# Four of sixteen x chunks transposed by TensorE instead of by the load, in a two-branch state-space kernel with a written-out order

## The chip, the cores and the metric

The kernel runs on one core of one Trainium2 chip. The metric is the time of one execution on the device in microseconds (us); of several executions the median is given. A difference of about 0.5% is what a measurement of this kernel can tell from no change.

## The reference

Two state-space layers over the same length S = 2048 and width D = 1024 are computed from separate inputs and set side by side in one output of 2048 x 2048.

```python
# branch A: short convolution of k, gate by v, long convolution, gate by q
kv = k_shift * v                      # k_shift: 4 shifted copies of k, weighted and summed
y  = irfft(rfft(kv, 2*S) * rfft(ssm_k, 2*S))[:S] + kv * ssm_D
a  = q * y
# branch B: diagonal complex recurrence
Bu = einsum("bld,pd->blp", x, B_bar)  # B_bar from Lambda, log_dt, B_re, B_im
for t in range(L): h = Lam_bar * h + Bu[:, t]; hs.append(h)
b  = 2 * einsum("blp,dp->bld", hs, Cmat).real + x * Dskip
out = concatenate([a, b], axis=-1)
```

## The kernel before

**One order for everything.** The kernel's work is cut into about 1,500 small tasks. A string, `ORDER`, names them one after the other, and the program walks through it (the loop over `ORDER.split()` at the end of `full_kernel`): each word calls the function of that task, which issues its instructions. Each engine takes its own instructions in this order, so the string sets five queues at once: TensorE, VectorE, ScalarE, GpSimd (half of the stores and swaps) and SyncE (all loads, some stores). A word such as `x.12:a52` is task x for chunk 12, into the working memory from unit 52 on; p is a PSUM bank, h one of three slots of the state, w one of three slots of weights. A task waits for its data and for what lay in its place before.

**Branch B** goes in 16 chunks of 128 time steps. Task x loads a chunk of x with a transposing DMA on SyncE (line 447), so that the width lies on the partitions. U (line 464) multiplies it with the tables BT, made at the start from B by transposes on TensorE (bT, line 415, 128 x 128 each, eight to a tile, against an identity) and a copy out of PSUM. ue copies U out of PSUM. VectorE then rotates (r1, line 487; r2, 498), scans twice (sc, 504), rotates back (r3, 487; r4, 510). cy carries the last column to the next chunk. y (line 520) or its form in four quarters yq (538) multiplies with CT and adds x * Dskip with one small matmul from the same transposed chunk; ye (556) copies out, and a store follows. Eight pieces of CT come by transposing loads (line 437), eight by TensorE and a copy on ScalarE (439).

**Branch A** does the long convolution as a Fourier transform in stages. am and hm are the first stages for kv and the filter; their results go to memory and come back re-sorted (lh, lk, line 676) as 16 units. For each unit stage 2 needs a table of weights, loaded by lw (line 671) into one of three slots `wslot`: sh and sk (line 687) read it first, and sa (line 725) last, after the product pr on VectorE (713) and the swap of rows sw or swp (707). Results are stored, come back (vl, 741), go through a3 (753), are copied out (a3e, 760), multiplied by q (qm, 762) and stored (763 on GpSimd, 764 on SyncE).

Most copies out of PSUM can stand on ScalarE or, with a v at the end of the task's name, on VectorE.

Of the kernel before, what the change touches and what calls it, by code (L numbers as in the profile page):

```python
# [16 lines left out]
BF16 = mybir.dt.bfloat16  # L17
# [55 lines left out]
ue.1.0:a34 bl.3.1:a19 bc.4.0 U.0.0.0:p5 U.0.0.1 bl.7.0:a41 bT.2.1:p4 bl.6.1:a12 U.0.2.0:p0 bT.3.1:p7 bc.5.0 U.0.2.1
bT.7.0:p6 stt ue.0.0:a24 bl.7.1:a20 bc.2.0 bc.2.1 x.2:a52 bT.6.1:p2 bT.7.1:p3 cl.1.0:a15 kp.-2 bT.3.0:p4 bc.7.0 kring
bc.3.1 x.3:a21 bc.3.0 U.1.2.1:p5 bc.7.1 U.1.2.0 cl.1.1:a37 U.1.1.1:p1 bc.6.1 U.1.1.0 cl.3.1:a14 U.0.3.1:p4 ue.0.2 ue.1.2
kvm.1:a16 z2 kvm.2:a42 U.0.3.0 rta kva.1 kva.2 z1 U.0.1.0:p7 kvb.1:a39 cT.1.0:p6 U.3.0.1:p3 ue.0.3 kvb.2:a12 U.0.1.1
ue.0.1 cc.1.0 cT.3.1:p0 vp.1:a27 kvm.0:a16 cl.0.1:a48 kvb.3:a26 kva.0 kvc.3 cc.3.1 ld_Q ue.1.1 vp.0:a40 kvb.0:a36
U.3.0.0 cx.5.1 cl.2.0:a13 U.3.2.0:p5 am.3.1:p7p2 ae.3.1.1:a19 r1.0:a29 kvc.2 U.3.2.1 ae.3.0.1 cl.0.0:a47 am.3.0:p6p4
cx.7.0 kvc.1 ae.3.1.0 ae.3.0.0 cT.1.1:p1 cl.2.1:a44 cT.0.1:p0 cT.0.0:p7 U.3.1.1:p2 cc.1.1 cx.6.0 U.3.3.1:p4 cl.3.0:a42
ue.3.2:a46 kp.2 cT.2.1:p5 U.3.1.0 gz r2.0:h1 kvc.0 ue.3.0 sc.0.0 sc.0.1 am.2.1:p1p3 cc.0.0 U.1.3.0:p7 cc.0.1 hl.0.1:a23  # L80
cT.3.0:p6 r3.0:a27 ue.3.1 U.3.3.0 ae.2.0.1:a40 U.1.3.1 cc.2.1 cc.3.0 U.2.0.1:p2 hl.1.0:a48 ae.2.1.1 am.0.0:p0p3 ue.3.3
ue.1.3 ae.0.0.0:a43 ae.0.1.0 am.0.1:p4p5 ae.0.1.1 r1.3:a15 U.2.0.0 ue.2.0:a36 am.1.1:p0p6 hl.0.0 r4.0 U.2.2.0:p1 hl.1.1
ae.0.0.1 ast.0 am.1.0:p2p7 ae.1.0.1:a45 U.2.2.1 cx.6.1 r2.3:h2 ast.3 hT.0.1:p4 r1.1:a27 hT.0.6:p3 ae.1.1.0 U.2.3.1:p7
kvm.4:a14 ae.1.1.1 ue.2.2 cx.4.1 ae.1.0.0 r2.1:h0 hd.0 am.2.0:p6p5 hc.0.1:a22 U.2.3.0 ae.2.1.0 ast.1 cx.7.1 hd.1 ue.2.3
cT.2.0:p1 ae.2.0.0 hT.0.3:p2 cc.2.0 hc.0.6:a32 U.2.1.0:p7 U.2.1.1 hc.0.3:a13 hT.0.7:p0 hm.0.6.1:p4p1 hT.0.4:p6 cx.4.0
cy.1 kva.4 y.0.0.0:p3 ue.2.1 ast.2 sc.1.1 hc.0.4:a28 sc.1.0 hc.0.7:a12 y.0.0.1 hm.0.4.0:p2p6 kvb.4:a31 he.0.6.1.0:a43
he.0.4.0.1:a29 he.0.4.0.0 he.0.6.1.1 hT.0.0:p5 cx.5.0 hT.0.5:p0 vp.2:a34 y.0.0.2 hT.0.2:p1 r3.1:a45 hc.0.0:a19
hm.0.6.0:p6p2 he.0.6.0.0 hm.0.4.1:p5p4 he.0.4.1.1 he.0.4.1.0 y.0.0.3 hst.0.6.1 y.0.1.0:p6 kp.3 ye.0.0:a25 hc.0.5:a14
kvc.4 hst.0.4.1 y.0.1.1 he.0.6.0.1 r4.1 y.0.1.2 hm.0.0.1:p0p5 hc.0.2:a20 hm.0.7.0:p4p7 he.0.7.0.1:a50 y.0.1.3 r1.2:a15
hst.0.4.0 he.0.0.1.1:a48 hm.0.0.0:p2p3 hm.0.5.1:p7p5 y.1.1.0:p1 hst.0.6.0 he.0.7.0.0 kvm.6:a38 he.0.0.1.0 he.0.0.0.1  # L90
y.1.1.1 he.0.5.1.0:a23 he.0.0.0.0 hm.0.5.0:p4p2 he.0.5.1.1 he.0.5.0.1 vp.3:a26 am.4.0:p0p7 ye.0.1 he.0.5.0.0
ae.4.1.0:a29 x.4:a32 kp.4 y.1.1.2 y.1.1.3 y.1.0.0:p6 r2.2:h1 ae.4.0.0 kva.6 hm.0.7.1:p0p3 ye.1.1:a28 hst.0.7.0
hm.0.3.0:p2p5 hm.0.3.1:p7p4 y.1.0.1 kvm.5:a14 he.0.7.1.0 ysp.0 he.0.7.1.1 am.4.1:p1p0 cy.2 kvb.6:a19 kva.5 kvc.6
he.0.3.1.1:a36 y.1.0.2 he.0.3.1.0 kvb.5:a25 hst.0.0.1 he.0.3.0.0 hm.0.1.0:p3p2 hl.2.0:a44 sc.2.1 hst.0.5.1 hl.2.1
# [24 lines left out]
ye.4.1:a11 kva.14 U.6.2.1:p1 kvc.13 am.13.1:p6p0 cy.5:h1 kva.12 ye.4.0 kvb.14:a3 lw.0:w0 ae.11.1.0 am.13.0:p5p3
ae.13.1.1:a9 kvc.15 U.8.3.0:p2 ae.13.0.0 ast.10 lh.3:a5 kvc.14 ae.11.0.0 ae.13.1.0 kvb.12:a20 ae.13.0.1 U.6.2.0  # L120
am.15.0:p3p0 am.14.1:p7p5 ae.14.0.1:a21 ae.15.0.0:a34 ae.15.1.0 U.8.3.1 ast.11 U.7.2.1:p4 r1.5:a45 ue.6.2 ae.14.1.1
am.15.1:p3p0 ae.15.1.1 kvc.12 am.14.0:p1p7 ast.13 ae.15.0.1 ae.14.1.0 x.10:a26 U.7.2.0 ae.14.0.0 r2.5 am.12.1:p5p0
lh.1:a32 ae.12.1.1:a45 U.9.0.1:p7 ae.12.0.1 am.12.0:p6p3 ae.12.1.0 ae.12.0.0 r1.6:a41 ue.7.2 ue.8.3:a38 U.9.0.0
ue.9.0:a30 U.8.1.1:p3 sc.5.0 sh.2:p5p4 sh.3:p0p1 she.3.0:a47 sc.5.1 she.2.1 ast.14 sh.7:p2p6 she.3.1 lh.0:a0 U.8.1.0
she.2.0 r2.6:h2 U.9.1.0:p0 U.8.2.0:p4 ysp.4 she.7.0:a11 she.7.1 ue.8.1 U.9.1.1 sh.1:p6p1 ast.12 sh.6:p7p5 sh.0:p2p3
# [63 lines left out]
def full_kernel(ctx, tc, A_q, A_k, A_v, A_shift_k, A_ssm_k, A_ssm_D, B_x, B_Lre, B_Lim, B_Bre, B_Bim,  # L189
                B_Cre, B_Cim, B_log_dt, B_Dskip, out):  # L190
    nc = tc.nc
# [252 lines left out]
    def x_(i):  # L444
        nm = "xm" if i in bounced else "xT"
        st[nm, i] = sb(1).rearrange("p (d t) -> p d t", d=ND)
        nc.sync.dma_start_transpose(st[nm, i], x[i * T:(i + 1) * T, :])
# [394 lines left out]
```

## Time and profile before

| what | us |
|---|---|
| three timed runs | 351.01, 348.97, 350.45; median 350.45 |
| profiled execution, whole | 352.94 |
| its span, first to last instruction | 351.0 |
| TensorE busy in the span | 332.9 |
| VectorE busy | 326.1 |
| ScalarE busy | 273.4 |
| mean granted clock of TensorE | 0.989 |

The profile is one execution. PE is TensorE, PEld its weight load, DVE VectorE, ACT ScalarE, POOL GpSimd, and SP (or SPq, its queue) SyncE. An x with a number counts instructions. A window's row gives its length, the busy time and count of each engine, the granted clock of TensorE, the mean busy share of the 16 DMA engines (packets that overlap can bring it over 1) and what they moved in GB/s. A row of the timeline gives start and length of a group of like instructions, and in brackets the idle time ahead of it and what ended that. A row of the waits gives us in all, times, and the longest.

### The profile page before, as it was taken

How to read it: one execution, taken by the hardware profiler on the slowest of the kernel's cores; microseconds unless marked ns; L12 is line 12 of the kernel's file. 1: busy time of each engine (PE TensorE's matmuls, PEld its weight loads, DVE VectorE, ACT ScalarE, POOL GpSimd, SP SyncE). 2: the span in 40 equal slices, each digit the busy share in tenths (PEclk: the TensorE clock that was granted, in tenths of full speed). 3: DMA queues.
4: the chain of work that ended last, by engine and by line, in shares of the span. 5: the costliest groups of instructions: out<-in, count | busy, mean ns of one | idle time of the engine just before them, and what ended most of it. 6: DMA issues, size and time to landing. Idle time of an engine off the chain costs nothing. (4 is left out here: it accounts for less than half of the span.)

```text
span 351.0 us, 11815 instructions
## 1 busy us (share of the span) xinstructions
PE 332.9 (95%) x5105; PEld 233.2 (66%) x5105; DVE 326.1 (93%) x261; ACT 273.4 (78%) x524; POOL 68.0 (19%) x110
## 2 busy tenths in 40 slices
PE   5989999999999999999999989999699999999991
PEld 2789888547856886689665565765575887754440
DVE  4999999999999999999999989999779999999961
ACT  6999999999999973798889769999378974235640
POOL 6000011343422552120111210031021122000020
PEclk9999999999999999999999999999899999999997
DMA  5999999898996888968998999898978898798996
GB/s 193 357 286 293 278 264 324 271 288 329 279 327 211 319 283 234 324 233 307 308 244 293 194 357 357 309 236 250 292 264 301 288 314 310 229 381 273 366 326 226
DMA packets 62880, 101.09 MB, mean 288 GB/s; under 512 B 29422, under 2 KB 31742, under 8 KB 62828
## 3 DMA queue, kind: packets, MB, share of 16 engines
q1 hardware_dynamic: 53228, 67.39, 66.1%
q0 software_dynamic: 9600, 32.95, 25.9%
q8 instruction: 40, 0.66, 0.8%
q14 instruction: 12, 0.10, 0.1%
HBM read 52.08 MB, written 33.55 MB: 244 GB/s over the span
## 5 line engine op out<-in xcount | busy, mean ns | idle before, releaser
L464 PEld LDWEIGHTS <-BT 128*128 128x128 bf16 x2048 | 118.4, 99 | 13.7 <-issue 9.2
L464 PE MATMUL bank<-arena,BT 128*128 128x128 bf16 x2048 | 126.0, 221 | 0.3 <-ACT BT L431 0.3
L538 PE MATMUL bank<-CT,gslot 64*64 64x512 bf16 x1408 | 88.2, 378 | 0.1
L504 DVE TENSOR_TENSOR_SCAN gslot<-rtab,gslot 128x1040 bf16<-128x1040 f32 x32 | 72.9, 2310 | 0.7
L538 PEld LDWEIGHTS <-gslot 64*64 64x64 bf16 x1408 | 38.8, 107 | 29.4 <-issue 1.4
L473 ACT CAST arena<-bank 128x512 bf16<-128x512 f32 x61 | 37.2, 642 | 14.0 <-PE bank L464 13.0
L613 ACT CAST arena<-bank 128x512 bf16<-128x512 f32 x64 | 36.6, 658 | 8.0 <-PE bank L607 5.3
L520 PE MATMUL bank<-CT,gslot 128*128 128x512 bf16 x160 | 39.4, 379 | 0.0
L696 ACT CAST arena<-bank 128x512 bf16<-128x512 f32 x62 | 33.4, 615 | 7.3 <-PE bank L687 5.7
L713 DVE TENSOR_TENSOR arena<-arena 128x4096 bf16<-128x4096 bf16 x16 | 36.5, 2285 | 2.3 <-ACT arena L473 1.6
L487 DVE TENSOR_TENSOR arena<-gslot,Z 128x4096 bf16<-128x4096 bf16 x16 | 36.6, 2288 | 0.9 <-PE bank L687 0.4
L703 ACT CAST arena<-bank 128x512 bf16<-128x512 f32 x60 | 33.7, 609 | 4.0 <-PE bank L687 2.6
L487 DVE TENSOR_TENSOR arena<-arena,Z 128x4096 bf16<-128x4096 bf16 x16 | 36.5, 2283 | 0.0
L733 ACT CAST arena<-bank 128x512 bf16<-128x512 f32 x60 | 32.7, 615 | 4.4 <-PE bank L725 4.4
L664 ACT CAST arena<-bank 128x512 bf16<-128x512 f32 x64 | 34.6, 635 | 1.7 <-PE bank L656 1.6
L587 DVE TENSOR_TENSOR arena<-arena 128x4096 bf16<-128x4096 bf16 (+3 forms) x16 | 29.9, 1880 | 0.0
L667 POOL DMA_DIRECT2D Ys_h<-arena x32 | 23.5, 737 | 28.6 <-ACT arena L664 26.1
L616 POOL DMA_DIRECT2D Ys_kv<-arena x16 | 11.1, 711 | 87.2 <-ACT arena L613 86.1
L687 PE MATMUL bank<-arena,wslot 64*64 64x512 bf16 x256 | 22.1, 383 | 4.7 <-DMA wslot<-a_c_W 4.7
L556 ACT CAST arena<-bank 128x512 bf16<-128x512 f32 x31 | 18.3, 601 | 9.9 <-PE bank L523 4.4
L760 ACT CAST arena<-bank 128x512 bf16<-128x512 f32 x26 | 13.6, 600 | 15.6 <-PE bank L753 15.6
L520 PEld LDWEIGHTS <-gslot 128*128 128x128 bf16 x160 | 14.4, 98 | 16.1 <-issue 1.5
(104 smaller groups left out, 416.8 us busy)
## 6 DMA issues: line engine op xcount, KB each, us to landing
Ys_kv<-arena POOLq DMA_DIRECT2D x16, 512.0 KB, 5.0
Ys_h<-arena POOLq DMA_DIRECT2D x32, 256.0 KB, 4.7
arena<-Ys_h SPq DMA_DIRECT2D x16, 512.0 KB, 7.2
arena<-Ys_kv SPq DMA_DIRECT2D x16, 512.0 KB, 5.4
Vs<-arena POOLq DMA_DIRECT2D x16, 512.0 KB, 5.7
arena<-Vs SPq DMA_DIRECT2D x16, 512.0 KB, 7.5
arena<-in_A_k_dram SPq DMA_DIRECT2D x8, 512.0 KB, 6.3
arena<-in_A_v_dram SPq DMA_DIRECT2D x8, 512.0 KB, 4.7
```

The source lines that it names most:

```text
L464: nc.tensor.matmul(pu[:, w, jl, :], BT[:, 2 * jp + jl, w, d, :], xT[:, d, :], start=(d == 0), stop=(d == ND - 1))
L473: cp(st["u", i][:, :, 2 * jp:2 * jp + 2, :], st.pop(("pu", i, jp)))
L487: nc.vector.tensor_mul(m, s_, win(Z))
L504: nc.vector.tensor_tensor_scan(gf, rtab[:].rearrange("p j t -> p (j t)"), gf, 0.0, ALU.mult, ALU.add)
L520: nc.tensor.matmul(py, h[:, w, j, 2:GW], CT[:, j, w, dh * 512:(dh + 1) * 512], start=(j == 0 and w == 0), stop=False)
L538: mm = nc.tensor.matmul(st["py", i, dh][cols, cs(r)], lhs(dh, rows, c), rhs(dh, rows), start=first, stop=last)
L613: cp(st["ysb", n2][:, p, dh * 512:(dh + 1) * 512], st.pop(("pa", n2, p, dh)))
L664: cp(o, st.pop(("pb", hf, s, e, r)).rearrange("p (n c t) -> p n c t", n=2, c=2))
L696: cp(st["hab", i][:, 0, a, l, :], st.pop(("ps", "h", g, l)))
L703: cp(st["x16", i][:, a, l, :], st.pop(("ps", "k", g, l)))
L713: nc.vector.tensor_mul(hab, st.pop(("x16", i)).rearrange("p a l d -> p (a l d)").unsqueeze(1).to_broadcast([P, 2, 2 * D]), hab)
L733: cp(st["vsb", i][:, a, dh * 512:(dh + 1) * 512], st.pop(("pv", g, dh)))
```

## The change

Chunks 11, 12, 13 and 14 of x are no longer loaded with a transposing DMA. A plain load on SyncE (xn, 256 KB) brings each in, eight transposes on TensorE (xt, the helper `tr_` at line 415 that also serves bT) turn it into one PSUM bank, and one copy on ScalarE (xc) brings it to its place. The other twelve chunks and the eight pieces of CT keep their transposing loads. An unused path (xs, xl) is taken out.

```diff
-    bounced = set(map(int, re.findall(r"\bxl\.(\d+)", ORDER)))
-    xd = {i: tc.dram_tile([P, D], BF16, name="xd%d" % i) for i in sorted(bounced)}
     def x_(i):
-        nm = "xm" if i in bounced else "xT"
-        st[nm, i] = sb(1).rearrange("p (d t) -> p d t", d=ND)
-        nc.sync.dma_start_transpose(st[nm, i], x[i * T:(i + 1) * T, :])
+        st["xT", i] = sb(1).rearrange("p (d t) -> p d t", d=ND)
+        nc.sync.dma_start_transpose(st["xT", i], x[i * T:(i + 1) * T, :])
     E["x"] = x_
-    E["xs"] = lambda i: gpd(xd[i], st.pop(("xm", i)).rearrange("p d t -> p (d t)"))
-    def xl(i):
-        st["xT", i] = sb(1).rearrange("p (d t) -> p d t", d=ND)
-        spd(st["xT", i].rearrange("p d t -> p (d t)"), xd[i])
-    E["xl"] = xl
+    def xn(i):
+        st["xn", i] = sb(1)
+        spd(st["xn", i], x[i * T:(i + 1) * T, :])
+    E["xn"] = xn
+    E["xt"] = lambda i: tr_(("xn", i), ("xp", i))
...
+    def xc(cp, i):
+        st["xT", i] = sb(1).rearrange("p (d t) -> p d t", d=ND)
+        cp(st["xT", i], st.pop(("xp", i)))
+    either("xc", xc)
...
-U.11.2.1 she.18.0 ysp.8 she.19.0 she.18.1 sw.9.0 x.13:a31 lw.11:w1 lh.14:a34 sk.19:p0p3 yq.9.4 ue.11.2 sh.23:p2p1
+xt.13:p2 xc.13:a45 ysp.7 vst.6 yq.9.4 swp.7.0 sh.19:p3p6 she.19.1 r4.10 sk.19:p5p4 swp.7.1 lw.11:w0 vst.8 she.19.0 pr.7
```

The string `ORDER` is another throughout, in order and in the places in memory. Besides the twelve new tasks, the counts that changed are these: six more copies out of PSUM stand on VectorE and six fewer on ScalarE (he, sae, ske, a3e and ye moved to VectorE in part, she and ue back to ScalarE by one each); six of the 32 swaps of rows went from SyncE to GpSimd; and some stores changed between the same two queues. Three places show how the order moved.

First, SyncE's queue at the start, up to the first transposing load of x. The load of the five parameter rows (praw) ends just ahead of these rows; in the changed kernel one more load of k stands ahead of them. Before:

```order
L273 DMA praw<-in_A_ssm_D_dram 8x128
L420 DMA arena<-in_B_B_re_dram 128x1024 x2
L420 DMA arena<-in_B_B_im_dram 128x1024
L420 DMA arena<-in_B_B_re_dram 128x1024
L420 DMA arena<-in_B_B_im_dram 128x1024
L420 DMA arena<-in_B_B_re_dram 128x1024
L447 DMA_TRANSPOSE arena<-in_B_x_dram 128x8x128
```

And with the change:

```order
L273 DMA praw<-in_A_ssm_D_dram 8x128
L571 DMA arena<-in_A_k_dram 128x2048
L420 DMA arena<-in_B_B_re_dram 128x1024 x2
L420 DMA arena<-in_B_B_im_dram 128x1024
L420 DMA arena<-in_B_B_re_dram 128x1024
L420 DMA arena<-in_B_B_im_dram 128x1024
L420 DMA arena<-in_B_B_re_dram 128x1024 x5
L420 DMA arena<-in_B_B_im_dram 128x1024 x3
L443 DMA_TRANSPOSE arena<-in_B_x_dram 128x8x128
```

The first transposing load moved behind two loads of k and seven more loads of B. On TensorE eleven tiles of B are now transposed ahead of the first U, seven before.

Second, SyncE's queue where the tables of weights of units 11, 10 and 15 are loaded (wslot; Ys_h and Ys_kv are the first stages' results, arena to arena is a swap of rows). Before, with the transposing loads of chunks 13 and 12:

```order
L447 DMA_TRANSPOSE arena_95<-in_B_x_dram 128x8x128
L671 DMA wslot1_93<-a_c_W3 128x640
L676 DMA arena_95<-Ys_h_87 128x2x1024 x3
L447 DMA_TRANSPOSE arena_95<-in_B_x_dram 128x8x128
L671 DMA wslot0_92<-a_c_W3 128x640
L671 DMA wslot2_94<-a_c_W3 128x640
L676 DMA arena_95<-Ys_h_87 128x2x1024
L676 DMA arena_95<-Ys_kv_86 128x2x1024 x3
```

And with the change, where chunk 12 comes by the plain load of the first row and chunk 13 has come earlier:

```order
L448 DMA arena_95<-in_B_x_dram 128x1024
L565 DMA out_0_dram<-arena_95 128x1024
L708 DMA arena_95<-arena_95 64x2048 x2
L672 DMA wslot0_92<-a_c_W3 128x640
L677 DMA arena_95<-Ys_h_87 128x2x1024
L708 DMA arena_95<-arena_95 64x2048
L677 DMA arena_95<-Ys_kv_86 128x2x1024
L672 DMA wslot2_94<-a_c_W3 128x640
L677 DMA arena_95<-Ys_h_87 128x2x1024
L672 DMA wslot1_93<-a_c_W3 128x640
```

No transposing load stands among these rows any more. That of chunk 15 stays: it stood behind the table loads of units 12 and 14 and ahead of that of unit 13, and now stands behind that of unit 12 and ahead of those of 14 and 13.

Third, the end of VectorE's queue: the last scans and rotations (chunk 15), copies out of PSUM and products with q. Before:

```order
L487 TENSOR_TENSOR arena_95<-gslot1_90,Z2_78 128x4096
L762 TENSOR_TENSOR arena_95<-arena_95 128x2048 x2
L760 CAST arena_95<-bank7_103 128x512
L510 TENSOR_TENSOR gslot1_90<-arena_95 128x16x128
L760 CAST arena_95<-bank3_99 128x512
L762 TENSOR_TENSOR arena_95<-arena_95 128x2048 x2
L760 CAST arena_95<-bank2_98 128x512
L762 TENSOR_TENSOR arena_95<-arena_95 128x2048 x2
```

And with the change:

```order
L488 TENSOR_TENSOR arena_95<-gslot2_91,Z2_78 128x4096
L761 CAST arena_95<-bank1_97 128x512
L511 TENSOR_TENSOR gslot2_91<-arena_95 128x16x128
L763 TENSOR_TENSOR arena_95<-arena_95 128x2048 x2
L557 CAST arena_95<-bank2_98 128x512
L763 TENSOR_TENSOR arena_95<-arena_95 128x2048
L761 CAST arena_95<-bank3_99 128x512
L761 CAST arena_95<-bank1_97 128x512
L763 TENSOR_TENSOR arena_95<-arena_95 128x2048
L761 CAST arena_95<-bank6_102 128x512
L763 TENSOR_TENSOR arena_95<-arena_95 128x2048
```

The last r4 (line 510 before, 511 after) has fewer products ahead of it; five products and four copies now stand behind it, four and two before. On TensorE one group of a3 is left behind that r4, four before.

More of the change, by code (lines that the diff above doesn't have):

```diff
@@ L73 @@
[L73 to L82, printed above, removed]
@@ new lines @@
+r1.15:a27 r2.15:h2 a3.13.0:p0 a3.13.1:p4 a3e.13.1:a20 a3.7.0:p3 vl.9:a39 sc.14.1 a3.8.1:p6 a3.8.0:p4 vl.1:a13
+a3e.7.0:a49 a3.12.0:p3 yst.12 a3e.12.0 vl.2:a51 r3.14:a1 yq.13.4 r4.14 yq.13.5 yq.13.6 yq.13.7 a3e.13.0 vl.4:a43
+a3.9.0:p0 a3ev.8.0:a24 a3e.8.1 a3.12.1:p3 vl.0:a8 ye.13.1:a48 a3.1.0:p1 a3ev.12.1 cy.15 a3.0.1:p6 a3e.9.0 a3.2.0:p4
+a3.9.1:p7 a3e.9.1 a3.1.1:p0 sc.15.1 a3.0.0:p3 vl.3:a10 vl.10:a34 ye.13.0 vl.5:a26 a3.7.1:p7 vl.15:a1 vl.6:a28 vl.14:a30
+y.14.0.0:p5 a3e.1.1:a32 a3e.7.1 vl.11:a3 sc.15.0 y.14.0.1 a3.2.1:p0 a3e.0.1 qm.6 a3ev.0.0 a3e.1.0 qm.0 a3e.2.0:a8
@@ L186 @@
+osp.2 ysh.15.0 qm.7 y.15.1.0:p2 y.15.1.1 y.15.1.2 y.15.1.3 ost.7 ye.15.1 ysh.15.1
 """
```

220 lines of the change are left out of this document (112 added, 108 removed).

## The prediction

> **What bounds the kernel now.** I read the page's first part, then windows of 10 us, then the waits inside the weak windows.
>
> ```profile
> span 351.0 us, 11815 instructions
> PE 332.9 (95%) x5105; PEld 233.2 (66%) x5105; DVE 326.1 (93%) x261; ACT 273.4 (78%) x524; POOL 68.0 (19%) x110
> core 0: us, PE busy (x) PEld busy (x) DVE busy (x) ACT busy (x) POOL busy (x), PEclk, DMA share, GB/s
> 0.00:10.00 10.00, 5.97 (x26) 2.48 (x27) 5.01 (x16) 6.97 (x12) 5.63 (x17) 1.00 0.68 195
> 10.00:20.00 10.00, 9.49 (x124) 9.16 (x124) 9.62 (x25) 9.90 (x24) 0.00 (x0) 1.00 1.08 362
> 120.00:130.00 10.00, 10.00 (x168) 8.86 (x162) 10.00 (x8) 7.65 (x16) 6.22 (x10) 1.00 0.88 312
> 200.00:210.00 10.00, 9.09 (x161) 6.96 (x156) 8.36 (x6) 7.71 (x16) 1.46 (x2) 1.00 1.05 318
> 240.00:250.00 10.00, 7.55 (x160) 4.47 (x152) 8.25 (x5) 7.37 (x16) 1.08 (x2) 1.00 0.93 207
> 250.00:260.00 10.00, 9.26 (x128) 7.57 (x128) 8.64 (x5) 4.88 (x10) 1.83 (x3) 0.83 0.80 284
> 260.00:270.00 10.00, 10.00 (x208) 6.59 (x208) 7.80 (x6) 9.10 (x18) 2.04 (x3) 1.00 0.91 330
> 340.00:350.00 10.00, 3.99 (x23) 1.79 (x20) 3.77 (x4) 1.17 (x2) 1.45 (x2) 0.85 0.75 285
> ```
>
> TensorE and VectorE are both full in a window such as 120 to 130: whoever wants time must find it on both. Time is lost at the head, between 200 and 270, and in the tail. In the middle VectorE idles 1.64 + 1.75 + 1.36 + 2.20 = 6.95 us. TensorE loses there by three waits, all of stage 2 for its table of weights (wslot):
>
> ```profile
> 186.96 0.41 PE L687 MATMUL bank<-arena,wslot 64*64 64x512 bf16 x4 [0.22 <-DMA wslot<-a_c_W]
> 210.41 0.41 PE L687 MATMUL bank<-arena,wslot 64*64 64x512 bf16 x4 [1.32 <-DMA wslot<-a_c_W]
> 250.74 0.63 PE L687 MATMUL bank<-arena,wslot 64*64 64x512 bf16 x8 [3.19 <-DMA wslot<-a_c_W]
> ...
> 193.41 1.98 SPq L447 DMA_TRANSPOSE arena<-in_B_x_dram  x1
> 198.83 0.34 SPq L671 DMA_DIRECT2D wslot<-a_c_W  x1
> 240.78 1.27 SPq L447 DMA_TRANSPOSE arena<-in_B_x_dram  x1
> 243.02 1.32 SPq L671 DMA_DIRECT2D wslot<-a_c_W  x2
> ...
> SPq L671 <- PE bank L725: 22.1, 10, 5.3
> ```
>
> The longer two end 210.41 - 198.83 = 11.6 and 250.74 - 243.02 = 7.7 us after their loads were issued, and a transposing load of x (chunks 11 and 12) stands just ahead of each on SyncE. Those loads can't be issued earlier: SyncE waits 22.1 us for TensorE's last reads (L725) of the old table. What a transposing load does to the queues stands in windows of 2 us:
>
> ```profile
> 206.00:208.00 2.00, 2.00 (x41) 1.54 (x42) 2.00 (x2) 2.00 (x6) 0.00 (x0) 1.00 1.05 407
> 228.00:230.00 2.00, 2.00 (x50) 1.14 (x40) 1.90 (x3) 1.60 (x5) 0.00 (x0) 1.00 1.47 290
> 230.00:232.00 2.00, 2.00 (x52) 1.43 (x41) 2.00 (x1) 2.00 (x5) 0.00 (x0) 1.00 0.82 55
> 244.00:246.00 2.00, 2.00 (x49) 1.36 (x45) 1.97 (x2) 1.98 (x5) 0.00 (x0) 1.00 1.25 177
> 246.00:248.00 2.00, 1.55 (x36) 0.90 (x28) 1.90 (x2) 0.96 (x3) 0.00 (x0) 1.00 0.99 112
> 250.00:252.00 2.00, 1.26 (x15) 0.85 (x16) 0.74 (x2) 0.58 (x2) 0.00 (x0) 0.83 1.09 390
> 252.00:254.00 2.00, 2.00 (x22) 2.00 (x20) 2.00 (x1) 0.49 (x2) 0.00 (x0) 0.50 1.02 374
> 254.00:256.00 2.00, 2.00 (x29) 1.40 (x27) 2.00 (x2) 1.08 (x3) 0.00 (x0) 0.81 0.30 111
> ```
>
> With plain transfers alone the DMA engines move 407 GB/s at a share of 1.05. Behind the transposing load of chunk 13 (228 to 232) they are busy (1.47 + 0.82) x 2 = 4.6 us and move 690 KB, which take 1.8 us at the plain rate; behind that of chunk 12 (244 to 248) 4.5 us for 578 KB, 1.5 us at the plain rate. So one costs the queues about 2.9 us more than a plain load. After the long wait the clock is granted at 0.83, 0.50 and 0.81: (0.17 + 0.50 + 0.19) x 2 = 1.7 us of TensorE.
>
> **The change part by part.**
>
> *Four transposing loads become plain ones.* The queues get back 4 x 2.9 = 11.6 us between 180 and 250. I let the three waits go whole: 0.22 + 1.32 + 3.19 = 4.73 us, and with the long one the slow clock, 1.7 us. Bounds: 0 (the loads are late anyway) and 6.4; I take 6.4, because the two long waits are the two with a transposing load close ahead and the order of after has a plain load there (chunk 12) or none. Late next would be the h and kv loads, which are issued further ahead.
>
> The Trainium skill, page "Advanced Engine Details and Errata", section "X-Bar Transpose (TRN2)", says the contrary: transposing DMAs on this chip are as fast as regular ones. The trace does not agree here, with 55 to 177 GB/s where plain transfers had 407. By the page this term would be 0 and only the costs below would remain.
>
> ```profile
> L415 PE MATMUL bank<-ident,arena 128*128 128x128 bf16 x192 | 16.0, 246 | 1.5 <-ACT arena L473 0.7 <-DMA arena<-in_B_B_re_dram 0.5 <-DMA arena<-in_B_B_im_dram 0.3
> L464 PE MATMUL bank<-arena,BT 128*128 128x128 bf16 x2048 | 126.0, 221 | 0.3 <-ACT BT L431 0.3
> L439 ACT COPY CT<-bank 128x1024 bf16<-128x1024 bf16 x8 | 8.6, 1183 | 0.0
> L760 DVE CAST arena<-bank 128x512 bf16<-128x512 f32 x6 | 4.0, 687 | 0.5 <-PE bank L753 0.4
> ```
>
> *32 transposes on TensorE.* The same function makes 192 in 16.0 us, 83 ns each: 32 x 83 = 2.7 us, on a full engine, so on the path. Low bound by the matmul row (126.0 / 2048 = 62 ns) 2.0; high bound 32 x 246 ns, each alone, 7.9.
>
> *Four copies on ScalarE*, 4 x 1.18 = 4.7 us. ScalarE is busy 7.4 to 7.7 of 10 us around 200 and 240; that idle time hides them, and a bank is held 1.2 us longer each. Without the cover up to 4.7 us; I take 0.
>
> *Evictions.* Six more stand on VectorE (6 x 0.687 = 4.1 us) and six fewer on ScalarE. By the order's tail, before has four products and two evictions behind the last r4, after five and four: 2 x 0.687 + 1.22 = 2.6 us of VectorE's work moved behind it. So ahead of it come 4.1 - 2.6 = 1.5 us more.
>
> ```profile
> 5.34 1.34 SPq L447 DMA_TRANSPOSE arena<-in_B_x_dram  x1
> 14.89 1.50 PE L464 MATMUL bank<-arena,BT 128*128 128x128 bf16 x16
> ...
> 333.34 1.22 DVE L510 TENSOR_TENSOR gslot<-arena 128x2048 bf16<-128x2048 bf16 x1
> 334.74 1.03 PE L520 MATMUL bank<-CT,gslot 128*128 128x512 bf16 x4
> 344.02 0.59 ACT L556 CAST arena<-bank 128x512 bf16<-128x512 f32 x1 [3.09 <-PE bank L523]
> 344.43 0.73 POOL L763 DMA_DIRECT2D out_dram<-arena  x1 [2.61 <-issue]
> ...
> arena<-in_B_x_dram SPq DMA_TRANSPOSE x16, 5.9
> ```
>
> *The tail.* The last r4 ends at 333.34 + 1.22 = 334.56, and the span 16.4 us later: TensorE needs 9.3 us for the rest of y and four groups of stage a3, then comes the copy at 344.02, and the store of 344.43. The order of after leaves one such group of four behind the last r4, so TensorE needs about 8 us there, and VectorE's own work (5 x 1.22 + 4 x 0.687 = 8.9 us) becomes the longer by a little: 9.3 - 8.9 = 0.4 us won on VectorE's side, nothing on TensorE's, whose groups only moved forward. Bounds: -1.3 and, if the products wait for q as one does before, +2.
>
> *The head.* SyncE now issues two loads of k and 13 of B ahead of the first transposing load of x (2 x 512 + 13 x 256 KB, 4.5 MB; before, six of B, 1.6 MB, and the issue at 5.34). At the 362 GB/s of 10 to 20 us that is 12 us, and with 5.9 us for the load the first U comes at 15 (the load's issue at about 9) to 18 us instead of 14.89. Before that U stand four more transposed B tiles than before (32 x 83 ns = 2.7 us), so up to 17.6 nothing is lost. Bounds: -2.7 and +11 (4.5 MB at the 195 GB/s of the first 10 us are 23 us, and 5.9 more). I take 0, by the nearer row.
>
> The rest of the order moved too. In 20 to 180 us neither engine has idle time to win; what a late load costs there has no row, and I take 0, with up to +2 in the range.
>
> **Sum.** TensorE: -4.73 - 1.72 + 2.66 = -3.8 us. VectorE: -6.95 + 1.5 - 0.4 = -5.9 us. The smaller gain sets the end: span 347.2, and the profiled execution 352.94 - 3.8 = 349.1. That execution lies 2.49 us above the median of the three timed ones (350.45). If this is the profiler's constant share, the median becomes 346.7; if its long wait and slow clock were that much worse than usual, only 1.3 us are left to win, 349.1. I take the middle, **347.9**; its own range is 345.0 to 349.6.
>
> **The rivals.**
>
> *VectorE alone sets the end* (13%). TensorE's ends are modelled, so its full windows may hold slack that swallows 32 transposes: 350.45 - 5.9 = 344.5. Against it: matmuls of U run at 62 ns without a gap.
>
> *The wait stays or moves* (16%). A table of weights is still asked for only when its slot is free. The load issued at 205.55 has no transposing load within 10 us ahead, and yet:
>
> ```profile
> 205.55 0.91 SPq L671 DMA_DIRECT2D wslot<-a_c_W  x1
> ...
> DMA to landing us min/median/max: 8.1/8.1/8.1
> ```
>
> And chunk 15 keeps its transposing load, in after ahead of two table loads instead of one. If half of 6.45 is won, -3.2 + 2.7 gives 349.9; if a wait like the longest returns behind chunk 15, -6.45 + 2.66 + 3.19 + 1.72 gives 351.6.
>
> *Transposing loads cost what plain ones do* (5%). The low GB/s rows would then come from what else was in flight; nothing is given back, the transposes are paid: 350.45 + 2.7 = 353.1. This is the outcome by the skill's page above.
>
> *The head is late* (12%), on the other side. Place: the first transposing load of x, behind 4.5 MB. Each us of the first U past 17.6 is a us of TensorE, which is full afterwards. From 17.6 + 2.5 = 20.1 us on it eats the gain against 350.45, from 21.9 on the kernel is slower by over 0.5%; with 22.6 it gives 352.9. For it: 195 GB/s in the first 10 us. Against: 362 right after.
>
> **How the numbers follow.** The forecast has 54%. A measurement can tell about 0.5%, 1.75 us: faster is under 348.7, slower over 352.2. Faster: 46 of the forecast's 54, and the 13 of VectorE's case, 59%. Same: 8 of the forecast, the 16 of the wait that stays, 3 of a mildly late head, 27%. Slower: 5 and 9, 14%. The range 344.2 to 351.6 reaches to both ends of the second rival and leaves out the third and most of the fourth.
>
> **What would show it.** Right: no wait for wslot over 0.5 us on TensorE between 180 and 270, the granted clock at 1.00 there, VectorE over 9.5 of 10 in the four windows, L415 with 224 matmuls and some 2.7 us more, no window of 2 us under 150 GB/s except behind chunk 15. Wrong: first U after 17.6; table loads landing later than 6 us with plain loads around them; new waits of VectorE for k or v before 180.

## The result, and the profile after

The changed kernel takes **352.33 us** (median of 20 runs, 350.09 to 355.14), the kernel before on the same chip 350.62 us (20 runs, 347.00 to 353.26). The ratio is 1.008 with a 95% interval of 1.0055 to 1.0105: slower by 0.8%, where 347.9 us and a gain were forecast. The ratio leaves out the longest executions of a kernel and the medians do not; by the medians the loss is 1.7 us, 0.5%. The profiled execution of the changed kernel took 353.03 us with a span of 351.3. Against the profiled execution of the kernel before (352.94) it seems to lose nothing; that one was a long one of its kind, 2.3 us above the median of the 20.

The page's first part, and the windows of 10 us that the prediction showed for the kernel before:

```profile
span 351.3 us, 11866 instructions
PE 330.4 (94%) x5118; PEld 233.1 (66%) x5137; DVE 329.4 (94%) x267; ACT 274.8 (78%) x522; POOL 69.9 (20%) x113
...
0.00:10.00 10.00, 3.71 (x9) 1.02 (x9) 2.70 (x18) 4.49 (x9) 5.64 (x17) 1.00 0.74 224
10.00:20.00 10.00, 7.21 (x89) 6.60 (x88) 9.69 (x17) 9.90 (x19) 0.00 (x0) 1.00 1.08 355
200.00:210.00 10.00, 9.89 (x196) 6.59 (x189) 9.90 (x6) 8.40 (x17) 3.17 (x5) 1.00 0.96 337
240.00:250.00 10.00, 9.97 (x208) 6.29 (x204) 9.97 (x7) 9.58 (x20) 2.42 (x4) 1.00 0.86 298
250.00:260.00 10.00, 10.00 (x190) 7.21 (x181) 10.00 (x7) 8.45 (x18) 2.40 (x4) 1.00 0.81 278
```

The middle is close to what was forecast: in these windows from 200 to 260 TensorE and VectorE are full, at a granted clock of 1.00, and TensorE waits for no table of weights. The head is worse: in the first 10 us TensorE does 3.71 us of work (5.97 before) and VectorE 2.70 (5.01).

VectorE's balance shows where the time went, since its busy time and its idle time make up the span. The windows of five stretches, the kernel before first, then the changed one (busy time of PE, PEld, DVE, ACT, POOL, then clock, DMA share and GB/s):

```profile
0.00:60.00 60.00, 54.49 (x774) 47.71 (x775) 54.60 (x80) 56.82 (x97) 8.43 (x21) 1.00 1.07 284
60.00:100.00 40.00, 40.00 (x394) 24.80 (x393) 40.00 (x30) 38.22 (x72) 13.69 (x19) 1.00 0.94 297
100.00:180.00 80.00, 80.00 (x1345) 58.89 (x1347) 79.93 (x60) 64.37 (x129) 21.30 (x31) 1.00 0.84 274
180.00:270.00 90.00, 85.12 (x1624) 55.45 (x1620) 82.24 (x45) 73.71 (x149) 15.42 (x25) 0.98 0.96 287
270.00:360.00 90.00, 73.33 (x988) 46.39 (x980) 69.36 (x50) 40.24 (x80) 9.16 (x14) 0.97 0.78 271
```

```profile
0.00:60.00 60.00, 49.29 (x721) 43.63 (x725) 52.22 (x78) 52.34 (x89) 7.75 (x20) 1.00 1.05 274
60.00:100.00 40.00, 37.80 (x399) 24.62 (x404) 37.66 (x29) 36.95 (x72) 11.98 (x17) 1.00 0.83 263
100.00:180.00 80.00, 78.82 (x1247) 58.71 (x1255) 78.95 (x60) 65.24 (x127) 22.90 (x34) 1.00 0.91 284
180.00:270.00 90.00, 89.87 (x1760) 59.38 (x1756) 88.24 (x51) 80.53 (x159) 16.80 (x27) 1.00 0.87 295
270.00:360.00 90.00, 74.61 (x1008) 46.74 (x1004) 72.29 (x53) 39.74 (x79) 10.48 (x16) 0.98 0.78 276
```

A window's length less the third busy time is VectorE's idle time there (the last window counts up to the end of the span). The same for the runs that follow, one profiled execution each, in us:

| kernel | 0-60 | 60-100 | 100-180 | 180-270 | 270-end | busy | span |
|---|---|---|---|---|---|---|---|
| before | 5.40 | 0.00 | 0.07 | 7.76 | 11.64 | 326.13 | 351.0 |
| before_again | 5.21 | 0.18 | 0.07 | 4.50 | 10.71 | 325.73 | 346.4 |
| after | 7.78 | 2.34 | 1.05 | 1.76 | 9.01 | 329.36 | 351.3 |
| old_order_plain | 5.75 | 0.05 | 0.07 | 5.59 | 11.41 | 326.23 | 349.1 |
| new_order_transposing | 7.76 | 2.09 | 0.17 | 5.16 | 10.45 | 329.67 | 355.3 |
| k_loads_later | 8.44 | 1.82 | 0.17 | 2.36 | 9.56 | 329.25 | 351.6 |
| r3_place | 8.37 | 2.15 | 0.17 | 2.37 | 9.68 | 329.66 | 352.4 |
| params_first | 6.49 | 4.43 | 0.17 | 1.42 | 9.53 | 329.66 | 351.7 |
| params_first_r3 | 6.66 | 3.65 | 0.65 | 1.42 | 10.21 | 329.61 | 352.2 |
| old_params_late | 8.69 | 0.21 | 0.07 | 3.49 | 10.80 | 325.54 | 348.8 |
| places_only | 7.78 | 0.03 | 0.17 | 1.74 | 9.06 | 329.12 | 347.9 |
| places_params | 6.99 | 0.10 | 0.68 | 1.74 | 9.43 | 329.46 | 348.4 |
| old_x12 | 5.28 | 0.16 | 0.13 | 2.41 | 11.58 | 325.84 | 345.4 |
| old_x12_13 | 5.19 | 0.21 | 0.07 | 3.11 | 11.92 | 325.70 | 346.2 |

From before to after: 6.0 us won from 180 to 270 and 2.6 in the tail, 3.2 us of work added; lost 2.4 in the head, 2.3 from 60 to 100 and 1.0 from 100 to 180. The sum is +0.3, the difference of the spans. This sets a long execution of the kernel before against one of the changed kernel that is close to its median. Against the second execution of the kernel before (before_again, 348.12 us) the same balance reads 2.7 us won from 180 to 270 and 1.7 in the tail, 3.6 of work added, and 2.6, 2.2 and 1.0 lost up to 180: +4.9. So the losses up to 180 are the same in both, and the gain of the middle depends on the execution.

The two largest losses have these rows. The kernel before, then the changed one:

```profile
4.43 0.20 DVE L284 CAST p<-bank 128x40 f32<-128x40 bf16 x1 [3.43 <-PE bank L279]
89.32 2.28 DVE L487 TENSOR_TENSOR arena<-gslot,Z 128x4096 bf16<-128x4096 bf16 x1
```

```profile
7.13 0.20 DVE L284 CAST p<-bank 128x40 f32<-128x40 bf16 x1 [6.13 <-PE bank L279]
12.42 1.34 SPq L443 DMA_TRANSPOSE arena<-in_B_x_dram  x1
20.70 1.07 PE L459 MATMUL bank<-arena,BT 128*128 128x128 bf16 x16 [1.20 <-DVE BT L429]
...
87.87 0.66 DVE L603 TENSOR_TENSOR arena<-arena 128x1024 bf16<-128x1024 bf16 x1
90.66 2.29 DVE L488 TENSOR_TENSOR arena<-gslot,Z 128x4096 bf16<-128x4096 bf16 x1 [2.13 <-PE bank L657]
```

The parameters' first use p (a copy on VectorE) stood at 4.43 before and now comes at 7.13, the first U at 20.70 instead of 14.89. VectorE's loss in the head is the wait for these parameters, 6.13 us instead of 3.43. And VectorE, full there before, stands 2.13 us ahead of the multiplication r3.2. The view names TensorE's bank as what ended that wait, but r3.2 writes to units 48 to 51, and 49 and 50 hold a tile (he.0.7) that two stores of Ys_h read. GpSimd's timeline, the kernel before and then the changed one, each with the time to landing of the stores of its row:

```profile
78.79 0.72 POOL L667 DMA_DIRECT2D Ys_h<-arena  x1 [1.70 <-ACT gslot L500]
...
DMA to landing us min/median/max: 6.2/6.2/6.2
```

```profile
81.81 2.17 POOL L668 DMA_DIRECT2D Ys_h<-arena  x3 [3.37 <-ACT arena L665]
...
DMA to landing us min/median/max: 7.3/7.8/8.0
```

By the order the row of 78.79 is the later of the two stores, and in the changed kernel both are the first two of the three of 81.81. Before, the store was issued 10.5 us ahead of r3.2 (89.32) and landed in 6.2. Now the two are issued some 6 us ahead of the time when VectorE is ready (88.5), and the stores of this row take 7.3 to 8.0 us to land: the second of the two, issued at about 82.5, lands after 90. Bank or store: the landing speaks for the store, and the experiments decide.

### The profile page after: what moved, and what is told of

It reads as the page before. It is cut to its first block, busy times and chain, and to the rows that moved or that the text cites. A ratio compares the mean times of both kernels' runs of the same rounds, so it can differ in the third digit from the quotient of the medians.

```text
span 351.3 us, 11866 instructions
## 1 busy us (share of the span) xinstructions
PE 330.4 (94%) x5118; PEld 233.1 (66%) x5137; DVE 329.4 (94%) x267; ACT 274.8 (78%) x522; POOL 69.9 (20%) x113
## 5 line engine op out<-in xcount | busy, mean ns | idle before, releaser
L459 PEld LDWEIGHTS <-BT 128*128 128x128 bf16 x2048 | 116.4, 98 | 15.8 <-issue 10.0
L459 PE MATMUL bank<-arena,BT 128*128 128x128 bf16 x2048 | 123.6, 219 | 2.5 <-DVE BT L429 1.2
L539 PEld LDWEIGHTS <-gslot 64*64 64x64 bf16 x1408 | 39.6, 107 | 28.2 <-ACT arena L704 1.5
L468 ACT CAST arena<-bank 128x512 bf16<-128x512 f32 x62 | 37.1, 625 | 16.2 <-PE bank L459 15.6
L521 PE MATMUL bank<-CT,gslot 128*128 128x512 bf16 x153 | 38.1, 379 | 0.8 <-issue 0.6
L697 ACT CAST arena<-bank 128x512 bf16<-128x512 f32 x63 | 34.5, 611 | 5.5 <-PE bank L688 5.3
L614 ACT CAST arena<-bank 128x512 bf16<-128x512 f32 x64 | 36.4, 632 | 2.9 <-PE bank L608 1.9
L665 ACT CAST arena<-bank 128x512 bf16<-128x512 f32 x63 | 35.2, 656 | 2.8 <-PE bank L657 2.5
L734 ACT CAST arena<-bank 128x512 bf16<-128x512 f32 x58 | 31.8, 603 | 4.1 <-PE bank L726 3.9
L704 ACT CAST arena<-bank 128x512 bf16<-128x512 f32 x58 | 32.5, 610 | 3.0 <-PE bank L688 2.7
L557 ACT CAST arena<-bank 128x512 bf16<-128x512 f32 x30 | 18.1, 623 | 15.6 <-PE bank L524 7.8
L708 POOL DMA_DIRECT2D arena<-arena x22 | 12.1, 549 | 50.7 <-ACT arena L697 35.7
```

The costliest lines, as they stand in the source:

```text
L459: nc.tensor.matmul(pu[:, w, jl, :], BT[:, 2 * jp + jl, w, d, :], xT[:, d, :], start=(d == 0), stop=(d == ND - 1))
L468: cp(st["u", i][:, :, 2 * jp:2 * jp + 2, :], st.pop(("pu", i, jp)))
L521: nc.tensor.matmul(py, h[:, w, j, 2:GW], CT[:, j, w, dh * 512:(dh + 1) * 512], start=(j == 0 and w == 0), stop=False)
L539: mm = nc.tensor.matmul(st["py", i, dh][cols, cs(r)], lhs(dh, rows, c), rhs(dh, rows), start=first, stop=last)
L614: cp(st["ysb", n2][:, p, dh * 512:(dh + 1) * 512], st.pop(("pa", n2, p, dh)))
L665: cp(o, st.pop(("pb", hf, s, e, r)).rearrange("p (n c t) -> p n c t", n=2, c=2))
```

## The experiments

Each group of runs had the kernel before beside it on the same chip. The groups, and the result above, are compared through that kernel: four chips served the four groups (the first four runs, the next four, the two with three places, the last two). Words in the cuts are those of `ORDER`, with remarks in brackets.

### The kernel before once more, and its order with four plain loads

The first run has no edit. The second moves nothing but the path of x:

```diff
-x.11:a14   x.12:a52   x.13:a31   x.14:a36
+xn.11:a14  xn.12:a52  xn.13:a31  xn.14:a36
+xt.14:p7 xc.14:a36   (ahead of yq.7.7)      xt.11:p7 xc.11:a14  (ahead of U.10.2.0)
+xt.13:p7 xc.13:a31   (ahead of yq.10.1)     xt.12:p4 xc.12:a52  (ahead of sc.11.1)
```

Expected of the kernel before again:

> The kernel before, unchanged, for a second profile and the granted clock of each run. Theory H (the new order loses at its start, and the middle gain is smaller in most executions than in the one profiled): the waits for wslot sum to under 3.5 us here (4.7 in the first profile), or the slow clock is missing (mean clock 0.994 or more, 0.989 in the first). Rival X (the x path itself costs; the middle loss of before is the usual one): waits of about 4.7 us and a clock near 0.989 again. Time about 350.6 either way.

Expected of its order with plain loads:

> The order of before, in which only chunks 11 to 14 of x come by a plain load at the old place, with the transposes and the copy put in before the chunk's first use. Theory H: the waits for wslot between 180 and 260 us shrink under 1.5 us, VectorE loses nothing at the start, and the time is 1 to 4 us under the kernel before (ratio 0.989 to 0.997). Rival X: 32 transposes and four copies on full engines make it slower by 1.5 to 3 us (ratio 1.004 to 1.009).

Measured: 348.7 us, ratio 0.9995 [0.9956, 1.0035], and 350.53 us, 1.0038 [1.0004, 1.0073]. TensorE's waits, the kernel before again first:

```profile
247.21 0.68 PE L687 MATMUL bank<-arena,wslot 64*64 64x512 bf16 x8 [1.97 <-DMA wslot<-a_c_W]
```

```profile
201.22 0.41 PE L688 MATMUL bank<-arena,wslot 64*64 64x512 bf16 x4 [0.57 <-ACT arena L704]
240.77 0.61 PE L415 MATMUL bank<-ident,arena 128*128 128x128 bf16 x8 [1.04 <-ACT arena L704]
251.38 1.95 PE L459 MATMUL bank<-arena,BT 128*128 128x128 bf16 x32 [0.54 <-ACT arena L474]
```

In the second execution of the kernel before, one wait of 1.97 us stands where the prediction's profile had three with 4.73 in all, as the theory had it. And in the old order the four plain loads remove the waits for wslot, but waits for ScalarE stand in their place, one of them for the copy xc itself (L474). The gain of 1 to 4 us did not come: alone, the new path of x gains nothing.

### The new order with transposing loads

```diff
-xn.11 xt.11 xc.11 xn.12 xt.12 xc.12 xn.13 xt.13 xc.13 xn.14 xt.14 xc.14
+x.11:a46 x.12:a44 x.13:a45   (each where xn stood)
+x.14:a36                     (behind lw.2)
```

> The order of the changed kernel with chunks 11 to 14 by transposing loads (chunk 14 a little later, where its place is free), without transposes on TensorE and copies. Theory H: waits for wslot of 2 us and more come back between 180 and 260 us, and the time is 1 to 4 us over the changed kernel's 352.3 (353 to 356). Rival X: 2 to 3 us are saved, 349 to 350.

Measured: 356.1 us, ratio 1.0189 [1.0137, 1.0241]. The waits are back:

```profile
184.85 3.00 SPq L443 DMA_TRANSPOSE arena<-in_B_x_dram  x2
187.95 0.53 SPq L672 DMA_DIRECT2D wslot<-a_c_W  x1
...
199.20 1.06 PE L688 MATMUL bank<-arena,wslot 64*64 64x512 bf16 x8 [2.28 <-DMA wslot<-a_c_W]
...
217.66 2.29 DVE L488 TENSOR_TENSOR arena<-arena,Z 128x4096 bf16<-128x4096 bf16 x1 [2.68 <-DMA Vs<-arena]
```

In the new order the plain loads are worth 1.9% - 0.8%, some 3.8 us: the path of x isn't the loss, the rest of the order is. Not all of the 3.8 us is the late table itself. VectorE's longest wait is the last row: the multiplication r1.9 writes to unit 33, which a store of Vs still reads, and that store was issued at 210.03 instead of 206.80 in the changed kernel.

### The loads of k later

```diff
-kp.1:a0 (ahead of the parameters)   kp.0 (ahead of seven loads of B)
+kp.1:a0 kp.0   (behind bl.1.0)
```

> The changed kernel with its first two loads of k moved behind the parameter rows and seven loads of B. Theory H, with the loads of k as the cause of the late start: the parameters reach VectorE at 4.4 to 5 us instead of 7.13, the second r4 is 1.5 us or more earlier (69.73 in the changed kernel, 67.86 before), the time 1 to 2.5 us under the changed kernel's. Rival (the order of the transposes and copies on TensorE and ScalarE sets the start): parameters earlier, but the first U and the second r4 within 0.5 us of the changed kernel's, time the same.

Measured: 353.9 us, ratio 1.0141 [1.0098, 1.0184]. p came at 5.65 instead of 7.13, and then

```profile
16.09 4.20 PE L415 MATMUL bank<-ident,arena 128*128 128x128 bf16 x40 [1.90 <-DMA arena<-in_B_B_re_dram]
24.71 2.85 PE L459 MATMUL bank<-arena,BT 128*128 128x128 bf16 x48 [2.19 <-DMA arena<-in_B_x_dram]
...
27.46 4.49 DVE L588 TENSOR_TENSOR arena<-arena 128x4096 bf16<-128x4096 bf16 x2 [2.30 <-DMA arena<-in_A_k_dram]
```

What is put later is waited for. Moving the two loads of k behind the parameters did not give the head's loss back.

### One place, and the parameters first

```diff
-r3.2:a48
+r3.2:a12
```

> The changed kernel with one tile moved: r3.2 writes to another piece of the arena that VectorE itself freed long before. Theory (VectorE stands about 2 us before r3.2 at 90.66 because its place is still being stored from): the idle time before r3.2 is under 0.5 us, VectorE is busy over 39.0 of the 40 us from 60 to 100 (37.66 in the changed kernel), the following r4 come about 2 us earlier, and the time falls by 1 to 2 us against 352.3. Rival (the wait is for TensorE's bank, whatever the place, or VectorE merely waits a few us later): the 2 us stand at the same place or at the next step, and the time is within 0.7 us of 352.3.

```diff
-kp.1:a0 ... ld_par ... par_T:p7 wbe.7 p32 exp1
+ld_par kp.1:a0 ...   and   wb.7:p0 par_T:p3 p32 exp1 ...
```

> The changed kernel with the parameters' load ahead of kp.1 on SyncE and their transposition and first step right behind the first w tile. Theory (the head lost about 2.3 us because the parameters land late): p starts at about 4.5 us instead of 7.13, the first U before 18.0 instead of 20.70, VectorE is busy over 9.0 of the first 15 us (7.56), and the time falls by 1.5 to 2.5 us. Rival (the loads share one rate and whatever is put first makes another late, as with the k loads put later): p is early but the second and third r4 are not, waits of 1.5 us or more for k, B or x appear from 15 to 30 us, and the time is within 0.7 us of 352.3 or above it.

Both edits together:

> The changed kernel with both edits: the parameters first and r3.2 in its other place. If both theories hold the gains add, 2.5 to 4.5 us: 348 to 350. If the head is lost again to other loads and only the place counts: 350.3 to 351.3. If neither: 352.3 within 0.7.

Measured: 354.94 us, ratio 1.0122 [1.0063, 1.018]; 351.6 us, 1.0048 [1.0011, 1.0086]; 353.33 us, 1.0102 [1.0061, 1.0144]. Neither theory came true as stated, and the sum did not add. The timelines show why. With r3.2 moved and nothing else, its wait is gone, so the place was what it waited for, and a later task of VectorE (kvm.7) waits instead:

```profile
97.45 2.29 DVE L588 TENSOR_TENSOR arena<-arena 128x4096 bf16<-128x4096 bf16 x1 [1.36 <-DMA Ys_kv<-arena]
```

ScalarE's copy hc.0.5 waits as well, 1.24 us in the changed kernel (first row). With the parameters first, p came at 4.41, and hc.0.5 waits 2.84 us, r3.2 1.97 (the other rows):

```profile
59.65 1.01 ACT L637 COPY arena<-bank 128x1024 bf16<-128x1024 bf16 x1 [1.24 <-DMA Ys_kv<-arena]
...
59.98 1.01 ACT L637 COPY arena<-bank 128x1024 bf16<-128x1024 bf16 x1 [2.84 <-DMA Ys_kv<-arena]
...
91.43 2.29 DVE L488 TENSOR_TENSOR arena<-gslot,Z 128x4096 bf16<-128x4096 bf16 x1 [1.97 <-DMA out_dram<-arena]
```

So three places in memory are taken again close behind a store that still reads them. Whoever repairs one of them, or arrives earlier, waits at the next; VectorE's idle time from 60 to 100 was 2.34 us in the changed kernel, 2.15 with r3.2 moved, 4.43 with the parameters first and 3.65 with both. That was the next theory.

### The old order with late parameters

```diff
-ld_par par_T p32 exp1 dve2 dve3   (at the start)
+ld_par par_T:p7 p32 exp1 dve2 dve3   (behind bl.1.0, four loads of B)
```

> The kernel before with one thing late: the parameters' load behind four loads of B, and their transposition and first two steps behind it. Theory (a delay of the head is carried to the end, since VectorE has next to no idle time after it): p starts 2 to 3 us later than 4.43, and the time rises by 1.5 to 2.5 us against the kernel before. Rival (the delay is absorbed by waits further on, so the head is free up to some us): the time is within 0.7 us of the kernel before.

Measured: 354.47 us, ratio 1.0108 [1.0049, 1.0168].

```profile
7.92 0.20 DVE L284 CAST p<-bank 128x40 f32<-128x40 bf16 x1 [6.92 <-PE bank L279]
```

p comes 3.5 us later than in the kernel before, the sixth r4 at 166.17 instead of 162.91, and the time rises by about 3.8 us (interval 1.7 to 5.9). In the old order a delay of the head is not absorbed: 3.3 of the 3.5 us still stand at the sixth r4, and the time rises by at least 1.7.

### All three places

```diff
-hc.0.5:a23   r3.2:a48   kvm.7:a13
+hc.0.5:a12   r3.2:a12   kvm.7:a12
```

> The changed kernel with three tiles moved to pieces of the arena that no running store reads: hc.0.5 (ScalarE's copy that stood 1.24 us before 59.65), r3.2 (2.13 us at 90.66) and kvm.7 (which stood 1.36 us at 97.45 when r3.2 alone was moved). Theory (the second loss of the new order is reuse of the arena close behind its stores, and a single place moved only hands the wait to the next one): no wait for a store over 0.5 us on VectorE or ScalarE from 55 to 100, VectorE busy over 39.2 of the 40 us from 60 to 100 (37.66), the r4 of the sixth tile at 167.5 or earlier (169.56), and the time 1 to 2.5 us below 352.3. Rival (from 60 to 100 the transfers or PSUM set the pace, and the wait comes up at a further place again): VectorE busy at most 38.3, the time within 0.7 us of 352.3 or above it.

And with the parameters first:

> The same three places together with the parameters' load first on SyncE and their transposition and first step right behind the first w tile. Theory (late parameters and reuse behind stores are the two losses of the new order): r4 of the sixth tile at 165.5 or earlier, VectorE busy over 39.2 from 60 to 100, and the time 347.5 to 349.5, no slower than the kernel before. Rival (as for the places alone): what the head gains stands at a store again, as it did with the parameters first alone, where ScalarE stood 2.84 us at 59.98: the time 351 to 353.

Measured: **350.01 us, ratio 0.9987 [0.9955, 1.0018]**, and 349.88 us, 1.0005 [0.9972, 1.0039]. The windows and r3.2 with the three places alone:

```profile
60.00:100.00 40.00, 39.37 (x422) 26.02 (x427) 39.97 (x30) 38.33 (x73) 14.38 (x20) 1.00 0.88 282
100.00:180.00 80.00, 79.58 (x1291) 58.95 (x1299) 79.83 (x60) 65.82 (x130) 20.45 (x30) 1.00 0.91 285
...
88.19 2.28 DVE L488 TENSOR_TENSOR arena<-gslot,Z 128x4096 bf16<-128x4096 bf16 x1
```

VectorE is full, r3.2 starts 2.47 us earlier than in the changed kernel (88.19 against 90.66), the third r4 2.48 us earlier (90.50 against 92.98), and the kernel is as fast as the one before. The places take 2.3 us of idle time from VectorE and 2.3 us from the time (352.33 to 350.01, with the kernel before at 350.62 both times): this covers what the changed kernel had lost. The bank's name at 90.66 misled; r3.2 waited for its place.

The sixth r4 is 3.45 us earlier (166.11 against 169.56), 1.0 more than the three places explain. In the changed kernel's profile VectorE had one more wait on the way:

```profile
158.08 2.29 DVE L488 TENSOR_TENSOR arena<-arena,Z 128x4096 bf16<-128x4096 bf16 x1 [0.87 <-ACT arena L614]
```

This is r1.5, which writes to units 15 to 18. The store of Ys_kv issued at 150.10 reads 15 and 16 and landed 7.9 us later, at 158.0. So it is a fourth place of the kind. It was left as it was in all seven runs of this order, and VectorE waited for it in only one of them (params_first_r3, 0.48 us); with the three places moved the same store landed in 5.3 us.

The parameters first gain nothing beside that, against the theory, which had them at 347.5 to 349.5 and the sixth r4 at 165.5 or earlier: it came at 166.19. With p 2.7 us earlier VectorE is only 0.8 us ahead at 60. It waits 1.33 us at 9.10 for a bank of TensorE, and then for other loads:

```profile
26.13 4.49 DVE L588 TENSOR_TENSOR arena<-arena 128x4096 bf16<-128x4096 bf16 x2 [0.73 <-DMA arena<-in_A_k_dram]
129.94 0.69 DVE L603 TENSOR_TENSOR arena<-arena 128x1024 bf16<-128x1024 bf16 x1 [0.51 <-DMA arena<-in_A_v_dram]
```

What order of the first loads would give the head's 2.4 us back was not found.

### The old order with one plain load, and with two

The path of x won nothing in the old order with four chunks. The longest wait of the kernel before stands behind chunk 12 alone, so that chunk was tried alone, transposed somewhat earlier than with all four:

```diff
-x.12:a52
+xn.12:a52
+xt.12:p7 xc.12:a52   (ahead of yq.10.7)
```

> The kernel before with one x tile alone, x.12, by a plain load, transposed ahead of yq.10.7 and copied by ScalarE. It is the load on SyncE right ahead of the two w loads that TensorE waited for at 250.74 (3.19 us) and 247.21 (1.97) in two profiled executions of the kernel before. Theory (this one transposing load makes the stall): no wait of TensorE for wslot over 0.5 us from 240 to 260, and with 0.67 us of transposes for it the time 1 to 2 us below the kernel before. Rival (the w loads are late for another reason, or the wait turns into one for ScalarE's copies as with all four): the time within 0.7 us of the kernel before.

The second run has chunk 13 as well (xt.13:p7 and xc.13:a31 ahead of yq.10.1):

> The same with x.13 as well, whose load stands ahead of a w load and three of Ys_h before it. Theory (each transposing load in front of w loads costs more than its eight transposes): 0 to 1 us below the run with x.12 alone. Rival (only x.12 stands on the path, and TensorE pays 0.67 us for each further tile): 0.3 to 1 us above it.

Measured: **346.81 us, ratio 0.988 [0.9831, 0.993]**, and 347.8 us, 0.9941 [0.9917, 0.9966]. The kernel before beside them took 350.06. With one chunk this is faster than both kernels of the study, by more than was expected (3.3 us by the medians, where 1 to 2 were expected). The windows, TensorE's one wait over 0.3 us from 180 to 270, and the landing times of the tables of weights:

```profile
180.00:270.00 90.00, 89.36 (x1739) 58.57 (x1727) 87.59 (x52) 79.88 (x162) 15.41 (x25) 1.00 0.93 300
...
246.00:248.00 2.00, 2.00 (x40) 1.19 (x40) 1.49 (x3) 1.97 (x4) 0.00 (x0) 1.00 1.04 390
...
245.35 0.62 PE L415 MATMUL bank<-ident,arena 128*128 128x128 bf16 x8 [0.64 <-DMA arena<-in_B_x_dram]
...
DMA to landing us min/median/max: 2.3/3.4/4.7
```

From 246 to 248, where the kernel before moved 112 GB/s at a DMA share of 0.99, it is now 390 at 1.04. Tables land within 4.7 us (8.1 at most in the first profile of the kernel before, 6.0 in the second), TensorE waits for none, and the six runs lie within 345.73 to 348.59, where the 17 of the kernel before spread from 347.54 to 353.83. With chunk 13 too, TensorE and VectorE wait again:

```profile
237.92 0.61 PE L415 MATMUL bank<-ident,arena 128*128 128x128 bf16 x8 [0.88 <-ACT arena L704]
247.88 0.69 DVE L697 CAST arena<-bank 128x512 bf16<-128x512 f32 x1 [1.69 <-PE bank L688]
```

The second run lies 1.0 us above the first, as the rival had it, though the two intervals overlap a little. So chunk 12's load is the one that stands on the path; making chunk 13's plain as well gained nothing and brought its transposes and a wait for a bank that ScalarE's copies (L704) had yet to empty. How much of the gain over the run with all four comes from transposing chunk 12 earlier was not separated.

## Why the prediction was wrong, step by step

**Four loads become plain, waits and clock go whole.** The mechanism was right: no wait for wslot over 0.5 us is left, the clock is 1.00, and undoing it in the new order costs 3.8 us. The size was off: this term, 6.4 us, is the price of one long execution. The second had waits of 1.97 us in all, and VectorE's idle time from 180 to 270 was 4.50 instead of 7.76 us. Half of the 2.49 us that the first lay above the median was taken for the profiler's constant share; the changed kernel's profiled execution lies 0.7 above its own median and the second of the kernel before 0.6 below, so most of it was the longer stall. In the old order four plain loads gained nothing, because waits for ScalarE took the place of those for wslot.

The Trainium skill, page "Advanced Engine Details and Errata", section "X-Bar Transpose (TRN2)", says that transposing DMAs are as fast as regular ones. The trace does not quite agree, though what else was in flight differs: in the changed kernel the transposing loads of x landed in 5.5 us (median of 12), the plain ones of the same size in 4.8 (median of 4). The 1.2% of the run with chunk 12 alone speak against it too.

**32 transposes and four copies.** There are 224 matmuls in the group against 192, and 4.2 us of copies against 4.7 counted:

```profile
L415 PE MATMUL bank<-ident,arena 128*128 128x128 bf16 x224 | 17.0, 232 | 2.8 <-ACT BT L431 1.9 <-ACT arena L408 0.8
L474 ACT COPY arena<-bank 128x1024 bf16<-128x1024 bf16 x4 | 4.2, 1046 | 0.0
```

The row rose by only 1.0 us over the 16.0 of before, but it holds two things: the 32 new transposes took 2.45 us between 180 and 260 (2.7 counted), and the 192 at the start 14.5 instead of 16.0. That the copies cost nothing holds in the new order only; in the old one they were waited for.

**Evictions and tail.** VectorE's busy time rose by 3.2 us (4.1 counted), and 2.6 us of its idle time behind 270 went, as the prediction had it. Taken with the 6.0 us of the middle, VectorE's own sum is -6.0 + 3.2 - 2.6 = -5.4 us, close to the -5.9 of the prediction; but that rests on the long execution of the kernel before. With the second one it is -2.7 + 3.6 - 1.7 = -0.8 us.

**The head, "I take 0, by the nearer row".** This step failed. The transposing load was issued at 12.42, not at about 9, and the first U came at 20.70, 3.1 us past the 17.6 up to which nothing should be lost. The head was also priced by the first U on TensorE alone, and VectorE's 2.4 us stand ahead of the parameters p, which have no term in the sum. The run with late parameters shows that a delay of this kind reaches the end, and putting the parameters first shows that they are not all of it: only 0.8 of the 2.4 us came back. The rival of the late head had the way to the end and a price of 1 us per us, which gives about 351 for a first U at 20.70; it looked at the load of x and not at the parameters, and its chance was too small.

**"The rest of the order moved too ... I take 0".** This step failed too, and it decides between slower and no change: VectorE lost 3.3 us from 60 to 180, of which other places for three tiles took back 2.3, and 0.9 stood at a fourth place that is not waited for in every execution. The waits at two of the three (hc.0.5 and r3.2) stood in the changed kernel's trace; the third (kvm.7) showed only once r3.2 was repaired. The two orders side by side held it: r3.2 keeps its units, but the two stores from there moved back among GpSimd's tasks, to 6 us ahead of it. The prediction read the order for queues and for tiles, not for who last reads a place.

**The signs given beforehand.** No wait for wslot, the clock and the 224 matmuls came true, and three of the four windows are full: VectorE has 8.95 of 10 us from 260 to 270. All three marks of the wrong case came in some form: the first U after 17.6, new waits of VectorE before 180, though for places and not for k or v, and one table that landed in 6.5 us (issued at 218.53, with plain loads around it), for which TensorE did not wait. The mark "no window of 2 us under 150 GB/s" was badly chosen: the changed kernel has six from 180 to 260, without any transposing load, such as

```profile
186.00:188.00 2.00, 2.00 (x52) 1.33 (x48) 2.00 (x2) 1.76 (x5) 0.00 (x0) 1.00 0.18 24
```

with a DMA share of 0.18: little was in flight. The 112 GB/s of the kernel before from 246 to 248 stood at a share of 0.99. The mark should have asked for the share too.

## What to carry to other kernels

Where an order or an allocation is made anew, look at which store last reads each place before a full engine writes it again; a repair at one such place can show nothing until the others are repaired too. A slow transfer matters only where a full engine waits behind it: in the old order one chunk, chosen by the chain from wait to load, gained about 1%, and all four gained nothing. Before a stall is priced from one execution, set that execution beside the others of the same kernel.

## What was not expected of the hardware

Executions of one kernel differ by much: those of the kernel before spread over 7.6 us on one chip (346.30 to 353.88), and its two profiled ones have 4.73 and 1.97 us of waits for tables of weights in the same order. With one transposing load gone, the six runs lie within 2.9 us. That these waits make the spread is not shown: the changed kernel has none of them, and its 20 runs spread over 5.1 us.

The same store takes different times to land in kernels of almost the same order: the one ahead of r1.5 took 7.9 us in the changed kernel and 5.3 with three places moved. And the view named three causes for the wait of r3.2 in runs of almost the same order (a bank of TensorE, a copy of ScalarE, a store of the output); the landing times and moving its place showed what it was.
